# Six score banks in three chunks, a VectorE tile inside a unit, and new priorities in a hand-scheduled attention and feed-forward kernel

The kernel runs on one core of one Trainium2 chip. The metric is device time in microseconds; lower is better.

## The reference

A pre-norm transformer block without learned norm weights: 2048 tokens, width 640, 32 heads of 20, full attention, then a gated feed-forward of 1728. Cut to what matters:

```python
qkv = (layernorm(x) @ wqkv)            # [2048, 3*640]
scores = q @ k.T * 20 ** -0.5          # 32 heads, each 2048 x 2048
o = softmax(scores) @ v
h = x + o @ wo
g, u = layernorm(h) @ w_gate, layernorm(h) @ w_up
out = h + (gelu(g) * u) @ w_down
```

## The kernel before

The program is not written in issue order. It records operations with an estimated duration, a priority, reads, writes and PSUM banks; a list scheduler then fixes the order of each engine, and that static order is compiled. The queries come in seven chunks (512, 512, 256, 256, 256, 128, 128). A "tile" is one 128x512 fp32 score bank; there are 2048. Tiles are taken in "units":

```python
PAT = [((0, 1, 2), (3, 4))] * len(CHUNKS)      # units of three and of two banks, in turn
...
qk = op("pe", fns, 0.215, P_QK, mode="row", ..., acq=bks)          # scores of a unit
xd = dtile[u]
if xd:                                          # one more tile, for VectorE, in a background bank
    bd = Bank(*BG[slots[xd[0]][0]])
    qd = op("pe", [...], 0.08, P_QK + 0.5, mode="row", ..., acq=[bd], after=[qk])
...
exp_ops.append(op("act", I("activation", pt, PS[...], ACT.Exp, scale=SCALE), c_act(n), P_QK,
                  mode="exp", reads=[("S", u)], writes=pk, rel=bks[0:na], ...))
```

ScalarE takes one exp over a whole unit. About one tile in eight goes to VectorE instead, which evicts it from PSUM and forms its exp by a chain of seven cheap operations for each pair of tiles. Softmax needs no maximum pass, because a bound is folded into the QK.

The output projection, layer norm and feed-forward of a chunk are "background": they run on TensorE and VectorE between the QKs and PVs of later chunks, with the lowest priorities, and their gelus interrupt ScalarE once a chunk. What is left of them, and the last chunk's whole feed-forward, runs in a tail behind the last exp.

In the profiles, before / after the change: line 852 / 873 is QK, 1039 / 1061 gate and up, 1096 / 1118 down, 616 / 630 other projections, 812 / 830 VectorE's eviction of its score tile. Line 339 / 353 is the helper through which exps, PVs and most of VectorE are recorded. The tiles tell them apart: `pts` and `rege` hold the probabilities.

Of the kernel before, what the change touches and what calls it, by code (L numbers as in the profile page):

```python
# [17 lines left out]
WARM_WIN, WARM_MIN = 3.4, 0.5  # L18
PAD_WIN, PAD_MIN = 3.4, 0.42
PE_AGE = 1.5  # L20

MODE_SWITCH = {"pe": 0.105, "act": 1.28}

# [18 lines left out]
class Sched:  # L42
# [3 lines left out]
    def __init__(self, nc):  # L46
        self.nc = nc
        self.ops = []
        self.lw = {}
        self.rd = {}  # L50
        self.warm = None
        self.pad = None
        self.final = set()

    def op(self, eng, fns, dur, prio, reads=(), writes=(), acq=(), rel=(), after=(), sem=None, lat=None, mode=None, util=0.0):
        o = Op()
        o.i = len(self.ops)
# [28 lines left out]
    def schedule(self):  # L86
# [18 lines left out]
        t = 0.0  # L105
        recent = collections.deque()
        live = False
        total = len(ops)
        while done < total:
# [4 lines left out]
            for e in ENGINES:  # L114
# [8 lines left out]
                while ready[e]:  # L123
                    p, i = heapq.heappop(ready[e])
                    o = ops[i]
                    got = []
                    for bk in o.acq:
                        for b in bk.allowed:
                            if owner[b] is None and free_at[b] <= t + 1e-9 and b not in got and b not in kept:
                                got.append(b)  # L130
                                break
                        else:
                            got = None
                            break
# [50 lines left out]
                if e == "pe" and self.pad is not None and o.tag and o.tag[0] == "O":  # L185
                    while recent and recent[0][0] < t - PAD_WIN:
                        recent.popleft()
                    u = sum(x for _, x in recent) + o.util
                    while u < PAD_MIN * PAD_WIN and o.util < 1.1:
                        o.fns = o.fns + self.pad  # L190
                        o.dur += 0.215
                        o.util += 0.213
                        u += 0.213
                    live = o.i not in self.final
                o.start = t
                if o.util:
                    recent.append((t, o.util))
# [87 lines left out]
S = 2048  # L285
# [23 lines left out]
ND = 4  # L309
D_PER_SLOT = (8,) * len(SIZES)  # L310
D_SLOT0 = 2
D_FIRST, D_SPAN = 1, 16
RSQRT_MAGIC = float(0x5F3759DF)

P_QK, P_PV, P_PRO, P_EPI, P_LN, P_BG = 0, 1, 1.5, 2, 2.5, 3


def bass_sequential_preLN__mha_block__glu_gated_geglu__prompt_kernel(
# [12 lines left out]
    with ExitStack() as es:  # L331
# [10 lines left out]
        def c_mm(n, passes=1):  # L342
            return 0.001 + passes * n / 2400.0

# [420 lines left out]

        PAT = [((0, 1, 2), (3, 4))] * len(CHUNKS)
        units, ubank, dtile, ends = [], [], [], []
        i, in_slot = 0, {}
        while i < len(tiles):
# [5 lines left out]
            units.append(tiles[i:i + len(bs)])  # L775
            ubank.append(bs[0])
            i += len(units[-1])
            want = min(nd, (k[0] - D_FIRST) * nd // D_SPAN + 1) if k[0] >= D_FIRST else 0
            if k[1] < want and tiles[i][0] == s_:
                dtile.append(tiles[i])  # L780
# [50 lines left out]
        def unit(u):  # L831
# [10 lines left out]
            pt = pb[:, 512 * o:512 * (o + na)]  # L842
            bks = [Bank(s0 + i) for i in range(len(tl))]
            fns = []
            reads = []
            nkm = max(512 // CHUNKS[slots[x[0]][0]][1] for x in tl)

# [15 lines left out]
            for kk in range(nkm):  # L863
                for i, x in enumerate(tl):
                    if kk < 512 // CHUNKS[slots[x[0]][0]][1]:
                        fns.append(qk_mms(lambda i=i: PS[:, 512 * (s0 + i):512 * (s0 + i) + 512], x, kk))
                        reads += qk_reads(x)
            qk = op("pe", fns, 0.215, P_QK, mode="row", util=0.0533 * len(tl), reads=reads, writes=[("S", u), "qkseq"], acq=bks)
            for x in tl:
                last_qk[slots[x[0]][0]].append(qk)  # L870
            xd = dtile[u]
            if xd:
                bd = Bank(*BG[slots[xd[0]][0]])
# [73 lines left out]
        def epilogue(s_, bk):  # L947
# [13 lines left out]
            for tt in range(4):  # L961
                op("pe", lambda eng, tt=tt: eng.transpose(bank(b2)[:, tt * 128:(tt + 1) * 128],
                                                          osb[:, s, tt * 128:(tt + 1) * 128], identf[:]),
                   c_mm(128, 4), P_EPI, mode="full", reads=[("osb", s), "identf"], writes=[key], acq=[b2] if tt == 0 else [],
                   after=tuple(aft) if tt == 0 else ())
            bv = lambda: bank(b2).rearrange("p (t j e) -> p t j e", t=4, j=4)
            rcv = rc[:, s, :].rearrange("p (t j) -> p t j", t=4)
            op("dve", lambda eng: eng.reciprocal(rcv, bv()[:, :, :, DH]), 0.17, P_EPI, reads=[key], writes=[("rc", s)])
            for gi, g in enumerate(gs):
# [3 lines left out]
                    rcv[:, gi * nt:(gi + 1) * nt, :].unsqueeze(3).to_broadcast([128, nt, 4, DH]), ALU.mult),  # L973
                   c_dve(80 * nt), P_EPI, reads=[key, ("rc", s)], writes=[("on", g, tb + tt) for tt in range(nt)],
                   rel=[b2] if gi == len(gs) - 1 else [])
# [146 lines left out]
        for s_, (c, gs) in enumerate(slots):  # L1122
# [30 lines left out]
            if gs[-1] == NG - 1:  # L1153
                tail = c == len(CHUNKS) - 1
                post(c, ALLB if tail else BG[c + 1], tail)
                if not tail:
                    prefetch(c + 1)
# [30 lines left out]
```

## Time and profile before

| | us |
|---|---|
| median of the four runs of before (lowest) | 928.55 (927.12) |
| median without the slow run | 927.77 |
| span of the profiled run | 925.5 |

One of the four runs, 1389.24 us, was slow; the ratios leave it out. Five terms add up to the span, and they follow from the start times of ScalarE's records:

- the time until the first exp;
- the exps, each counted with its usual distance from start to start;
- the lateness: what exps start later than that behind another exp;
- the breaks, in which ScalarE loads tables and does the gelus of a chunk;
- the tail, behind the slot of the last exp.

### The profile page before, as it was taken

The numbers are of one execution on the slowest core, as the hardware profiler recorded it, in microseconds if no ns is written. First come the engines' busy times: TensorE is split into PE (matmuls) and PEld (weight loads), VectorE is DVE, ScalarE is ACT, GpSimd is POOL, SyncE is SP. The second block draws the span as 40 slices with busy tenths as digits, with TensorE's granted clock in tenths as the row PEclk, the third lists the DMA queues.
The fourth block names the chain that finished last, engine by engine and source line by source line (L and its number), as shares of the span: only waits on it lengthen the run. The fifth ranks groups of instructions, "written<-read, shape, count | busy, mean of one in ns | idle before, by whom it ended". The sixth has DMA issues, their size and how long they took to land.

```text
span 925.5 us, 23154 instructions
## 1 busy us (share of the span) xinstructions
PE 845.3 (91%) x10109; PEld 354.8 (38%) x10109; DVE 810.3 (88%) x1703; ACT 885.7 (96%) x801; POOL 35.1 (4%) x117
## 2 busy tenths in 40 slices
PE   3998999999998998999888999999989999999998
PEld 2432322222232222233233333344444445555667
DVE  8859999999898998888798997989998997998873
ACT  6899999999999999999999999999999999999962
POOL 5000000000001000000001000001000000000100
DMA  7301010322550000001021000010100000110000
GB/s 256 95 18 44 18 55 18 90 60 66 152 180 16 15 1 1 1 15 44 1 31 23 9 2 1 16 30 10 37 16 16 9 23 2 31 32 10 10 17 16
DMA packets 39517, 34.36 MB, mean 37 GB/s; under 512 B 19436, under 2 KB 36936, under 8 KB 39416
## 3 DMA queue, kind: packets, MB, share of 16 engines
q1 hardware_dynamic: 39416, 32.89, 12.7%
q8 instruction: 79, 1.29, 0.6%
q14 instruction: 22, 0.18, 0.1%
HBM read 20.12 MB, written 8.09 MB: 30 GB/s over the span
## 4 chain that ended last, share of the span: by engine, by line
ACT 72%; PE 14%; DVE 11%; issue 1%; POOL 0%; DMA 0%
ACT pts L339 46%; ACT rege L339 25%; PE ps L1039 4%; DVE qt_all L339 3%; PE ps L616 3%; PE ps L852 3%; PE ps L339 3%; DVE rege L339 2%; PE ps L1096 2%; DVE qt_all L812 1%; DVE rege L812 1%; DVE stats L339 1%; ACT L339 1%; DVE rege L1074 1%; PE ps L561 0%
## 5 line engine op out<-in xcount | busy, mean ns | idle before, releaser
L339 ACT ACTIVATE pts<-ps 128x1536 bf16<-128x1536 f32 x480 | 573.1, 1379 | 4.9 <-PE ps L852 3.7
L852 PE MATMUL ps<-qt_all,kt_all 32*128 32x256 bf16 (+2 forms) x3584 | 303.4, 289 | 43.2 <-ACT pts L339 27.5
L339 ACT ACTIVATE rege<-ps 128x1536 bf16<-128x1536 f32 x239 | 300.1, 1381 | 2.1 <-PE ps L339 1.5
L852 PEld LDWEIGHTS ps<-qt_all,kt_all 32*128 32x128 bf16 x3584 | 95.0, 92 | 276.8 <-ACT pts L339 160.8
L339 DVE TENSOR_TENSOR qt_all<-qt_all 128x1024 bf16<-128x1024 bf16 (+1 forms) x240 | 164.0, 683 | 3.4
L1039 PE MATMUL ps<-rege,regw 128*128 128x256 bf16 (+2 forms) x980 | 154.7, 290 | 9.9 <-ACT rege L339 4.2
L339 PE MATMUL ps<-pts,v_all 128*21 128x256 bf16 (+2 forms) x2098 | 138.8, 290 | 0.5 <-DVE rege L339 0.5
L812 DVE TENSOR_SCALAR rege<-ps 128x512 int16<-128x512 f32 x154 | 105.3, 685 | 27.6 <-PE ps L852 26.8
L339 DVE TENSOR_SCALAR qt_all<-qt_all 128x1024 bf16<-128x1024 int16 (+1 forms) x288 | 115.8, 417 | 2.5
L339 PE MATMUL ps<-rege,v_all 128*21 128x256 bf16 (+2 forms) x1294 | 113.3, 292 | 0.1
L1039 PEld LDWEIGHTS ps<-rege,regw 128*128 128x128 bf16 x980 | 72.5, 98 | 67.9 <-issue 28.5
L616 PE MATMUL ps<-regw 128*128 128x512 bf16 (+1 forms) x360 | 86.9, 351 | 1.9 <-DVE v_all L749 0.7
L1096 PE MATMUL ps<-regw,rege 128*128 128x320 bf16 x448 | 79.4, 301 | 1.1 <-DVE rege L1064 0.5
L812 DVE TENSOR_SCALAR qt_all<-ps 128x512 int16<-128x512 f32 x96 | 65.6, 684 | 3.7 <-PE ps L852 2.6
L339 DVE TENSOR_SCALAR rege<-rege 128x1024 int16<-128x1024 int16 (+2 forms) x166 | 67.1, 421 | 1.3
L339 DVE TENSOR_TENSOR rege<-rege 128x1024 bf16<-128x1024 bf16 (+3 forms) x103 | 65.5, 644 | 0.9
L339 PEld LDWEIGHTS ps<-pts,v_all 128*21 128x21 bf16 x2098 | 50.2, 91 | 37.2 <-issue 31.6
L339 PE MATMUL ps<-kt_all,zer 128*32 128x512 bf16 x676 | 56.6, 384 | 0.0
L1096 PEld LDWEIGHTS ps<-regw,rege 128*128 128x128 bf16 x448 | 36.7, 97 | 32.4 <-issue 15.8
L339 PEld LDWEIGHTS ps<-rege,v_all 128*21 128x21 bf16 x1294 | 41.0, 91 | 20.6 <-issue 14.3
L1085 DVE TENSOR_TENSOR rege<-rege,ps 128x512 bf16<-128x512 bf16 (+1 forms) x53 | 35.7, 676 | 12.1 <-PE ps L1039 11.8
L616 PEld LDWEIGHTS ps<-regw 128*128 128x128 bf16 x360 | 28.6, 98 | 45.2 <-issue 21.0
(95 smaller groups left out, 574.3 us busy)
## 6 DMA issues: line engine op xcount, KB each, us to landing
rege<-in_A_x_dram SPq DMA_DIRECT2D x6, 640.0 KB, 5.1
q_rows<-regw SPq DMA_DIRECT2D x20, 128.0 KB, 1.7
out_dram<-rege SPq DMA_DIRECT2D x16, 160.0 KB, 2.1
regw<-in_B_w_gate_dram SPq DMA_DIRECT2D x1, 2160.0 KB, 11.9
regw<-in_B_w_up_dram SPq DMA_DIRECT2D x1, 2160.0 KB, 16.9
regw<-in_B_w_down_dram SPq DMA_DIRECT2D x1, 2080.0 KB, 22.9
kt_all<-k_rows SPq DMA_DIRECT2D x12, 160.0 KB
qt_all<-q_rows SPq DMA_DIRECT2D x12, 160.0 KB
```

Of the source, the lines that this page charges most:

```text
L339: return lambda eng: getattr(eng, method)(*args, **kwargs)
L616: yield op("pe", lambda eng, l=l, r=r, k=k: eng.matmul(bank(bk, n), l, r, start=(k == 0), stop=(k == len(steps) - 1)), c_mm(n), prio, mode ...
L812: d_ops.append(op("dve", lambda eng: eng.tensor_scalar(v[:, 512 * h:512 * h + 512], bank(b), EXP_MUL, -32000.0, ALU.mult, ALU.max), c_dve( ...
L852: return lambda eng: eng.matmul(out()[:, kk * nq:(kk + 1) * nq], kt_all[32 * j:32 * j + 32, g, kt * 128:(kt + 1) * 128], qt_all[32 * j:32 ...
L1039: op("pe", lambda eng, a=a, f=f, fi=fi: eng.matmul(bank(bk)[:, fi * nq:(fi + 1) * nq], w[:, a, F0[f]:F0[f] + 128], hnT[:, a, 128 * tb:128 ...
L1074: cp.append(op("dve", lambda eng, bg=bg, fv=fv, w=w: eng.tensor_copy(fv, bank(bg, w)), c_dve(w), p, reads=[kg], writes=hkeys(k), rel=[bg], ...
L1085: hdone.append(op("dve", lambda eng, bu=bu, fv=fv, w=w: eng.tensor_tensor(fv, fv, bank(bu, w), ALU.mult), c_dve(w), p, reads=[ku] + hkeys( ...
L1096: op("pe", lambda eng, f=f, o=o, hf=hf, bk=bk: eng.matmul(bank(bk, 320), ha_f[:, o:o + 128], wd[:, f, hf * 320:(hf + 1) * 320], start=(f = ...
```

## The change

Its intent: larger units in chunks two to four (six score banks, the VectorE tile being the third bank of a unit, one bank left for background work); quicker return of background banks, by putting the VectorE operations that free a bank (and the reciprocal and normalisation that lead up to one) ahead of its exp chains; no other TensorE work in front of a QK that falls due ("clearance"); 12 instead of 16 VectorE tiles in the last chunk; and three new cost figures in the scheduler. The core of the diff, cuts marked:

```diff
+QK_LEAD = .65
-MODE_SWITCH = {"pe": 0.105, "act": 1.28}
+MODE_SWITCH = {"pe": .098, "act": 1.28}
...
+        if eng == "dve" and rel and prio > self.ev:      # P_EV = 1.8 once the first chunk is through
+            prio = self.ev
...
+                    if e == "pe" and due is not None and o.prio[0] > 0 and t < due < t + o.dur + (...):
+                        skipped.append((p, i))
+                        ...
+                        continue
...
+                if e == "act":
+                    due = t + o.dur + (0.905 if o.dur > 1.2 else 1.332) - QK_LEAD if o.mode == "exp" else None
...
-D_PER_SLOT = (8,) * len(SIZES)
+D_PER_SLOT = (8,8,8,8,8,8,6)
...
-            return 0.001 + passes * n / 2400.0
+            return 0.004 + passes * n / 2400.0
...
-        PAT = [((0, 1, 2), (3, 4))] * len(CHUNKS)
+        PAT = [((0, 1, 2), (3, 4, 5)) if c in (1,2,3) else ((0, 1, 2), (3, 4)) for c in range(len(CHUNKS))]
...
+            if six and k[1] < want and len(units[-1]) == 3 and units[-1][2][0] == s_:
+                dtile.append(units[-1].pop())
...
-                   c_mm(128, 4), P_EPI, mode="full", ...
+                   c_mm(128, 2.5), P_EPI, mode="full", ...
```

More of the change, by code (lines that the diff above doesn't have):

```diff
@@ L53, in __init__ @@
         self.final = set()
+        self.ev = 9
     def op(self, eng, fns, dur, prio, reads=(), writes=(), acq=(), rel=(), after=(), sem=None, lat=None, mode=None, util=0.0):
+        if eng == "dve" and rel and prio > self.ev:
+            prio = self.ev
         o = Op()
@@ L107, in schedule @@
         live = False
+        due = None
         total = len(ops)
@@ L126, in schedule @@
                     got = []
+                    if e == "pe" and due is not None and o.prio[0] > 0 and t < due < t + o.dur + (MODE_SWITCH[e] if mode[e] not in (None, o.mode) else 0):
+                        skipped.append((p, i))
+                        if len(skipped) >= 60:
+                            break
+                        continue
                     for bk in o.acq:
@@ L188, in schedule @@
                     u = sum(x for _, x in recent) + o.util
-                    while u < PAD_MIN * PAD_WIN and o.util < 1.1:
+                    room = due - t - MODE_SWITCH[e] if due is not None and due > t else 1e9
+                    while u < PAD_MIN * PAD_WIN and o.util < 1.1 and o.dur + 0.215 < room:
                         o.fns = o.fns + self.pad
@@ L313 @@
 RSQRT_MAGIC = float(0x5F3759DF)
+P_EV = 1.8
 P_QK, P_PV, P_PRO, P_EPI, P_LN, P_BG = 0, 1, 1.5, 2, 2.5, 3
@@ L776, in bass_sequential_preLN__mha_block__glu_gated_geglu__prompt_kernel @@
             ubank.append(bs[0])
+            six = len(PAT[c][1]) == 3
             i += len(units[-1])
             want = min(nd, (k[0] - D_FIRST) * nd // D_SPAN + 1) if k[0] >= D_FIRST else 0
-            if k[1] < want and tiles[i][0] == s_:
+            if six and k[1] < want and len(units[-1]) == 3 and units[-1][2][0] == s_:
+                dtile.append(units[-1].pop())
+                k[1] += 1
+            elif not six and k[1] < want and tiles[i][0] == s_:
                 dtile.append(tiles[i])
@@ L842, in unit @@
             pt = pb[:, 512 * o:512 * (o + na)]
-            bks = [Bank(s0 + i) for i in range(len(tl))]
+            xd = dtile[u]
+            six = xd and len(PAT[slots[tl[0][0]][0]][1]) == 3
+            al = tl + ([xd] if six else [])
+            bks = [Bank(s0 + i) for i in range(len(al))]
             fns = []
             reads = []
-            nkm = max(512 // CHUNKS[slots[x[0]][0]][1] for x in tl)
+            nkm = max(512 // CHUNKS[slots[x[0]][0]][1] for x in al)
             def qk_mms(out, x, kk):
@@ L863, in unit @@
             for kk in range(nkm):
-                for i, x in enumerate(tl):
+                for i, x in enumerate(al):
                     if kk < 512 // CHUNKS[slots[x[0]][0]][1]:
@@ L867, in unit @@
                         reads += qk_reads(x)
-            qk = op("pe", fns, 0.215, P_QK, mode="row", util=0.0533 * len(tl), reads=reads, writes=[("S", u), "qkseq"], acq=bks)
-            for x in tl:
+            qk = op("pe", fns, 0.215, P_QK, mode="row", util=0.0533 * len(al), reads=reads, writes=[("S", u), "qkseq"] + ([("SD", xd)] if six else []), acq=bks)
+            for x in al:
                 last_qk[slots[x[0]][0]].append(qk)
-            xd = dtile[u]
-            if xd:
+            if six:
+                bd = bks[2]
+            elif xd:
                 bd = Bank(*BG[slots[xd[0]][0]])
@@ L963, in epilogue @@
                                                           osb[:, s, tt * 128:(tt + 1) * 128], identf[:]),
-                   c_mm(128, 4), P_EPI, mode="full", reads=[("osb", s), "identf"], writes=[key], acq=[b2] if tt == 0 else [],
+                   c_mm(128, 2.5), P_EPI, mode="full", reads=[("osb", s), "identf"], writes=[key], acq=[b2] if tt == 0 else [],
                    after=tuple(aft) if tt == 0 else ())
@@ L967, in epilogue @@
             rcv = rc[:, s, :].rearrange("p (t j) -> p t j", t=4)
-            op("dve", lambda eng: eng.reciprocal(rcv, bv()[:, :, :, DH]), 0.17, P_EPI, reads=[key], writes=[("rc", s)])
+            op("dve", lambda eng: eng.reciprocal(rcv, bv()[:, :, :, DH]), 0.17, min(P_EPI, sc.ev), reads=[key], writes=[("rc", s)])
             for gi, g in enumerate(gs):
@@ L973, in epilogue @@
                     rcv[:, gi * nt:(gi + 1) * nt, :].unsqueeze(3).to_broadcast([128, nt, 4, DH]), ALU.mult),
-                   c_dve(80 * nt), P_EPI, reads=[key, ("rc", s)], writes=[("on", g, tb + tt) for tt in range(nt)],
+                   c_dve(80 * nt), min(P_EPI, sc.ev), reads=[key, ("rc", s)], writes=[("on", g, tb + tt) for tt in range(nt)],
                    rel=[b2] if gi == len(gs) - 1 else [])
@@ L1154, in bass_sequential_preLN__mha_block__glu_gated_geglu__prompt_kernel @@
                 tail = c == len(CHUNKS) - 1
+                sc.ev = P_EV
                 post(c, ALLB if tail else BG[c + 1], tail)
```

## The prediction

> **What bounds the kernel now.** I read the busy table, the chain of work that ended last, the ScalarE groups by form, the waits, and then the timeline behind the last exp.
>
> ```profile
> PE 845.3 (91%) x10109; PEld 354.8 (38%) x10109; DVE 810.3 (88%) x1703; ACT 885.7 (96%) x801; POOL 35.1 (4%) x117
> ACT 72%; PE 14%; DVE 11%; issue 1%; POOL 0%; DMA 0%
> ...
> L339 ACT ACTIVATE pts<-ps 128x1536 bf16<-128x1536 f32 x240 | 381.5, 1589 | 4.4 <-PE ps L852 3.7 <-PE ps L339 0.6
> L339 ACT ACTIVATE pts<-ps 128x1024 bf16<-128x1024 f32 x240 | 280.5, 1169 | 0.5 <-PE ps L339 0.4
> L339 ACT ACTIVATE rege<-ps 128x1536 bf16<-128x1536 f32 x120 | 190.9, 1591 | 2.1 <-PE ps L339 1.5 <-PE ps L852 0.7
> L339 ACT ACTIVATE rege<-ps 128x1024 bf16<-128x1024 f32 x119 | 139.2, 1170 | 0.0
> ```
>
> ScalarE is busy 96% and holds 72% of the chain; it runs 360 exps of three score banks and 359 of two. The durations overlap their neighbours, so the cost is the distance between starts: in the trace's single records a three-bank exp is most often followed after 1331 ns and a two-bank one after 904 ns. That makes 427 ns a bank and 50 ns for each instruction (904 - 2 x 427). From the starts the span of 925.5 us divides without remainder into five terms:
> - before the first exp: 35.7 us
> - exps at those distances: 360 x 1.331 + 359 x 0.904 = 803.7 us
> - lateness of exps behind exps, beyond those distances: 12.9 us. Of it 10.1 us is in 42 places of over 0.05 us, the rest is jitter of some 16 ns
> - five breaks in which ScalarE changes tables and does the gelus of a chunk: 9.2 + 9.2 + 6.1 + 6.0 + 6.3 = 36.8 us
> - from the end of the last exp's slot, at 889.1, to the end: 36.4 us
>
> So most of the kernel is a saturated ScalarE. What can move is the lateness (12.9) and the tail (36.4). The tail is not ScalarE's:
>
> ```profile
> 830.00:889.10 59.10, 55.70 (x1273) 35.80 (x1260) 51.85 (x109) 59.04 (x52) 3.36 (x14) 1.00 0.05 11
> 889.10:925.50 36.40, 31.04 (x431) 25.79 (x428) 14.63 (x35) 11.32 (x15) 0.00 (x0) 1.00 0.04 15
> ```
>
> The columns are us, then TensorE, its weight loads, VectorE, ScalarE and GpSimd busy, clock and DMA. Before 889.1 ScalarE is full; after it, TensorE is busy 31.0 of 36.4 us. The timeline shows with what:
>
> ```profile
> 887.57 3.43 PE L1096 MATMUL ps<-regw,rege 128*128 128x320 bf16 x24
> ...
> 891.16 0.45 PE L339 MATMUL ps<-pts,v_all 128*21 128x128 bf16 x17
> ...
> 894.02 1.29 PE L1039 MATMUL ps<-rege,regw 128*128 128x128 bf16 x20 [0.34 <-DVE rege L1074]
> ...
> 897.85 1.45 PE L1039 MATMUL ps<-rege,regw 128*128 128x128 bf16 x23
> ...
> 900.49 1.70 ACT L339 ACTIVATE rege<-rege 128x1792 bf16<-128x1792 bf16 x1 [2.86 <-DVE rege L1074]
> ...
> 902.25 2.96 PE L1039 MATMUL ps<-rege,regw 128*128 128x128 bf16 x50
> ...
> 911.02 7.20 PE L1039 MATMUL ps<-rege,regw 128*128 128x128 bf16 x126
> 918.74 3.98 PE L1096 MATMUL ps<-regw,rege 128*128 128x320 bf16 x28 [0.52 <-DVE rege L1064]
> ```
>
> L1096 is a down projection, L1039 gate or up. 24 down matmuls left over from the fifth chunk stand in front of the last PV; then comes the whole feed-forward of the sixth chunk (70 gate, 70 up, 28 down), because its gate was not done in time, and then that of the last chunk (140 and 28). The sixth chunk's gelu starts only at 900.5, so its up projection occupies TensorE from 902.25 on.
>
> **What the Trainium skill says.**
> - "ScalarE: Activation LUTs", "What ACT_TABLE_LOAD costs": 0.833 ns per element; 186 ns fixed, of which neighbours overlap by about 93 ns; some 2.66 us for a change of set. The slope agrees (427/512 = 0.834 ns). The fixed part measures 50 ns, not 93, and a change about 1.5 us: the first break, 9.21 us, less gelus of 7168 columns (7168 x 0.834 ns + 4 x 50 ns = 6.18 us), leaves 3.03 us for two. I use the trace.
> - "PSUM — Partial Sum Buffer", "The four PSUM rules": eight banks, a matmul's output at most one bank of 512 fp32 columns. The 1536-column exps agree: three banks. Now 5 banks hold scores, 1 PV sums, 2 background work; after the change, in three chunks, 6, 1 and 1.
> - "Perfetto Trace Analysis", "Matmuls": independent groups should rotate through banks so that evacuating one overlaps the next group. One background bank gives that up for those chunks. No run shows that price yet.
> - "TensorE: Matmul & The Clock Gate", "Wait — 56ns, not 53.3ns?": N/2.4 GHz plus about 2.5 ns. It agrees: 126 matmuls of 128 columns in 7.20 us, (7.20 - 0.22)/125 = 55.8 ns; 28 of 320 in 3.98 us, (3.98 - 0.30)/27 = 136 ns.
>
> **The change part by part.** I counted in the issue orders of both built programs.
>
> (a) Three and three banks in the second to fourth chunk. 719 exps become 704: 394 of three banks and 310 of two. The VectorE tile is now a unit's third bank, so such a unit still has a two-bank exp. The last chunk gives VectorE 12 tiles instead of 16, so ScalarE gets 1802 banks instead of 1798. Sum: 394 x 1.331 + 310 x 0.904 = 804.7 us, **+1.0 us**: 15 instructions saved are 0.75, four banks more cost 1.7. The regrouping by itself is worth nothing that can be seen.
>
> (b) VectorE loses four evictions and two chains of seven steps, one for each pair of tiles; by the groups (685 ns an eviction, three steps at 0.68 and four at 0.42 a pair) some 9 us less of busy time, all in the last chunk. VectorE is not the bound; it only clears the last PV's inputs earlier.
>
> (c) Operations that free a bank now precede the exp polynomials on VectorE, from the first chunk's end on. With a queue 88% busy, that shortens the return of background banks. The orders show the sum of (a) to (c) on the background work: the fifth chunk's gelu now comes with 39 exps still to go instead of 27, and behind the last QK only about two matmuls of the sixth chunk's gate remain, and none of the fifth chunk's down. **Tail:** 24 x 0.136 + 70 x 0.056 = 3.3 + 3.9 = 7.2 us of TensorE work leave it. Are they on its path? Stepwise from the end E of the last exp: last PV 0.3 to 1.5, copy to 2.3, transposes and normalisation to 4.0, second transposes and their ScalarE eviction to 5.4, output projection to 7.0. Gelu needs one load and 1.7 us and is done by about 3 to 4, so the up projection (50 x 0.056 = 2.8) runs at 7 to 10 beside the layer norm; 28 down, 5 transposes and waits bring TensorE to about 14.2; then 140 x 0.056 = 7.9, a 0.5 us product, 28 x 0.136 = 3.8, and 2.8 us from the last matmul to the end as before: 29.2, say **29.5 us** against 36.4. One table load fewer (15 for 16) is in that. The gain is **-6.9 us**.
>
> (d) TensorE may not begin other work that would overrun a due QK. It aims at lateness such as the 0.37 us at 534.9, where 25 PV matmuls ran ahead of a QK. Against it, TensorE has more to do before E: work other than QK between QKs rises from 404 to 416 us by the counts (7.2 from the tail, some 4 us of fillers), and gaps between QKs holding over 0.75 us of work go from 155 to 189. I take 11 us for 12.9, **-1.9 us**.
>
> (e) Head and five breaks: the same instructions, so 35.7 and 36.8.
>
> Sum: 35.7 + 804.7 + 11 + 36.8 + 29.5 = 917.7 us of span. The profiled run before took 927.45 for a span of 925.5, 1.95 more, which gives 919.6; I say **919.5 us**, 1.1% below 929.32.
>
> **The rivals.**
> - *The single bank becomes the wait.* Matmuls into bank 7, eviction and return run in series, TensorE stands in order behind them, QKs come late. For it: the chunk-three gelu moves from 13 to 39 exps into the fifth chunk, so background work does lag there; and waits on evictions exist already (below). Against: the order places QKs between, and the work fits. At 0.1 us in a quarter of the 341 exps of those chunks it costs 8 us: 927.
>
> ```profile
> PEld ps L616 <- DVE rege L812: 5.7, 16, 0.7
> PEld ps L1039 <- DVE qt_all L812: 5.0, 13, 0.7
> DVE rege L812 <- PE ps L852: 26.8, 35, 3.5
> ```
>
> - *VectorE's third bank holds up the next QK.* The bank is free only after VectorE's eviction (0.685 us, behind an operation of up to 0.7), where before it was ScalarE's own. For: 128 units are of this kind. Against: the two-bank exp beside it lasts 0.9 and the next one 1.33, so there is slack of about one exp. If it failed, 128 x 0.05 us = 6 us: 925.
> - *The clearance rule works fully.* The 42 large places vanish and only 3 us of jitter stay: 911 to 912.
> - *The tail is bound by its chain, not by TensorE.* Then only half of the 7 us returns: 923.
>
> **Range and chances.** Tail 28 to 33 and lateness 4 to 16 give 911 to 928 at the extremes together; eight in ten is **913 to 926**. Faster by over 2% means under 910.7, which needs nearly all lateness gone besides the whole tail gain: 0.06. Slower by over 2% needs 948, some 28 us of new waits: 0.03. Within 2%: 0.91.
>
> **What would show it.** In the changed profile: 704 exps with starts 1331 and 904 ns apart; first exp at 35 to 36; last exp's end at 887 to 890, hardly moved; no 24 down matmuls ahead of the last PV, gelu of the sixth chunk within 5 us of the last exp, and a tail of 28 to 31 us; lateness 9 to 13 us. Wrong if lateness in chunks two to four grows beyond its present 5 us or so (single bank or VectorE bank), if the tail stays above 33, or if the last exp ends before 884, which would mean the clearance rule is worth more than I gave it.

## More of the kernel before

An exp writes probability tiles into a ring of buffers, which the PV matmuls read later:

```python
PR, PR2 = 12, 6                                 # probability buffers: 12 in pts, 6 in rege
...
if p0 < PR < p0 + na: p0 = PR                   # a unit does not straddle the two parts
if p0 + na > PR + PR2: p0 = 0
...
pv = op("pe", fns, 0.218 * len(quads), P_PV, mode="col", ..., reads=reads, writes=[("O", s_), "pvseq"])
```

## The result

The changed kernel took 923.94 us (median of 4 runs, 923.76 to 924.54) against 928.55 us. The ratio is 0.9957, with a 95% interval of 0.9937 to 0.9976: the same within 2%, but a clear gain of some 0.4%. Ratios here are the mean time of one kernel's fast runs over the mean of the other's fast runs of the same rounds, so they are not quite the ratios of the medians. The time lies in the predicted range; the gain is less than half of the 1.1% forecast. That 1.1% was taken from 929.32 us, the median of the three runs then known, of which one was the slow one; in spans of profiled runs, which leave this aside, 7.8 us were forecast and 3.7 came.

| us | before | after | difference | predicted difference |
|---|---|---|---|---|
| until the first exp | 35.7 | 36.3 | +0.6 | 0 |
| exps | 803.7 | 804.7 | +1.0 | +1.0 |
| lateness | 12.9 | 13.8 | +0.9 | -1.9 |
| breaks | 36.8 | 37.3 | +0.4 | 0 |
| tail | 36.4 | 29.8 | -6.6 | -6.9 |
| span | 925.5 | 921.8 | -3.7 | -7.8 |

From the page of the changed kernel, the busy table and the engines of the chain that ended last:

```profile
PE 821.2 (89%) x10080; PEld 351.1 (38%) x10141; DVE 805.5 (87%) x1685; ACT 885.8 (96%) x785; POOL 35.7 (4%) x117
...
ACT 70%; PE 16%; DVE 12%; issue 1%; DMA 1%; POOL 0%
```

ScalarE is as busy as it was (885.8 us against 885.7). Its groups by form, after (count, busy us, mean ns, idle before and who ended it):

```profile
L353 ACT ACTIVATE pts<-ps 128x1536 bf16<-128x1536 f32 x263 | 403.8, 1585 | 5.8 <-PE ps L873 4.5 <-PE ps L353 0.9
L353 ACT ACTIVATE pts<-ps 128x1024 bf16<-128x1024 f32 x211 | 243.0, 1152 | 0.2
```

With the other 131 and 99 these are the 394 and 310 exps that were counted. The tail changed as planned. The two windows, up to the last exp and from it to the end (columns as in the prediction):

```profile
832.60:892.00 59.40, 55.70 (x1255) 37.82 (x1257) 45.65 (x93) 58.33 (x51) 2.57 (x14) 1.00 0.05 14
892.00:921.80 29.80, 24.29 (x344) 20.20 (x345) 11.18 (x28) 9.96 (x14) 0.00 (x0) 1.00 0.04 13
```

TensorE has 24.3 us of work behind the last exp where it had 31.0. The timeline of the tail, after:

```profile
892.35 0.62 PE L353 MATMUL ps<-pts,v_all 128*21 128x128 bf16 x32 [1.42 <-ACT pts L353]
...
893.61 1.70 ACT L353 ACTIVATE rege<-rege 128x1792 bf16<-128x1792 bf16 x1
...
898.95 2.99 PE L1061 MATMUL ps<-rege,regw 128*128 128x128 bf16 x50
...
906.55 7.98 PE L1061 MATMUL ps<-rege,regw 128*128 128x128 bf16 x140
...
915.05 3.98 PE L1118 MATMUL ps<-regw,rege 128*128 128x320 bf16 x28 [0.52 <-DVE rege L1086]
```

The last PV starts 0.33 us after the last exp's slot, where 24 down matmuls had stood in front of it; the sixth chunk's gelu starts at 893.6, 1.6 us after it (11.4 us before: 900.5 less 889.1); no gate of the sixth chunk is left.

The lateness has to be looked at one exp at a time. For each exp at least 0.05 us late I matched the operations it waits for with their records: its own QK, and the PVs that last read the buffers that it overwrites. The later of them is what held it. Before, 39 late exps waited for their QK (6.9 us) and 4 for a PV (3.3 us); after, 47 for their QK (8.6 us) and 5 for a PV (3.7 us); what is left, 2.8 and 1.5 us, is in smaller pieces. The longest before was a wait for a PV, too, and stood in the timeline that was read for the prediction:

```profile
144.17 1.45 ACT L339 ACTIVATE rege<-ps 128x1536 bf16<-128x1536 f32 x1 [1.46 <-PE ps L339]
```

The longest after:

```profile
834.69 0.40 PE L873 MATMUL ps<-qt_all,kt_all 32*128 32x128 bf16 x12
...
835.70 0.39 PE L353 MATMUL ps<-rege,v_all 128*21 128x128 bf16 x8
836.03 0.40 PE L873 MATMUL ps<-qt_all,kt_all 32*128 32x128 bf16 x8
836.13 2.37 ACT L353 ACTIVATE pts<-ps 128x1536 bf16<-128x1536 f32 x2 [0.94 <-PE ps L353]
```

The scores were there at about 835.1, but the exp starts at 836.13, behind the PV that ends at 836.09. The releaser, line 353, is a PV and not a QK. By chunk the lateness, in us, is 5.0, 2.4, 2.3, 1.1, 1.2, 0.6, 0.3 before and 3.8, 2.9, 1.5, 0.9, 1.0, 1.8, 1.9 after. In chunks two to four, where the pattern changed, it fell a little in sum (though not in chunk two). It grew by 2.9 us in the last two chunks, where the work that left the tail now lies; 2.1 us of this are two exps, at 810.06 and 836.13, that wait for a slot's last PV of 48 matmuls.

### The profile page after: what moved, and what is told of

Its sections match the earlier page's. It is cut to its first block, busy times and chain, and to the rows that moved or that the text cites. A ratio compares the mean times of both kernels' runs of the same rounds, so it can differ in the third digit from the quotient of the medians.

```text
span 921.8 us, 23227 instructions
## 1 busy us (share of the span) xinstructions
PE 821.2 (89%) x10080; PEld 351.1 (38%) x10141; DVE 805.5 (87%) x1685; ACT 885.8 (96%) x785; POOL 35.7 (4%) x117
## 3 DMA queue, kind: packets, MB, share of 16 engines
q1 hardware_dynamic: 39416, 32.89, 12.9%
## 4 chain that ended last, share of the span: by engine, by line
ACT 70%; PE 16%; DVE 12%; issue 1%; DMA 1%; POOL 0%
ACT pts L353 44%; ACT rege L353 24%; PE ps L873 4%; DVE qt_all L353 4%; PE ps L353 3%; PE ps L630 3%; PE ps L1061 3%; PE ps L1118 2%; DVE rege L353 2%; ACT L353 1%; DVE rege L830 1%; DVE rege L1096 1%; DVE qt_all L830 1%; DVE stats L353 1%; PE ps L575 0%
## 5 line engine op out<-in xcount | busy, mean ns | idle before, releaser
L353 ACT ACTIVATE pts<-ps 128x1536 bf16<-128x1536 f32 (+1 forms) x474 | 574.7, 1392 | 6.0 <-PE ps L873 4.5
L873 PE MATMUL ps<-qt_all,kt_all 32*128 32x256 bf16 (+2 forms) x3584 | 287.7, 289 | 55.7 <-ACT pts L353 32.0
L353 ACT ACTIVATE rege<-ps 128x1536 bf16<-128x1536 f32 (+1 forms) x230 | 293.9, 1398 | 2.0 <-PE ps L353 1.2
L873 PEld LDWEIGHTS ps<-qt_all,kt_all 32*128 32x128 bf16 x3584 | 90.4, 92 | 276.9 <-ACT pts L353 163.6
L353 DVE TENSOR_TENSOR qt_all<-qt_all 128x1024 bf16<-128x1024 bf16 (+1 forms) x235 | 161.2, 686 | 4.1
L1061 PE MATMUL ps<-rege,regw 128*128 128x256 bf16 (+2 forms) x952 | 151.2, 287 | 14.8 <-ACT rege L353 4.7
L353 PE MATMUL ps<-pts,v_all 128*21 128x256 bf16 (+2 forms) x2122 | 136.1, 290 | 2.3 <-ACT pts L353 1.4
L353 PE MATMUL ps<-rege,v_all 128*21 128x256 bf16 (+2 forms) x1278 | 108.0, 292 | 0.0
L630 PE MATMUL ps<-regw 128*128 128x512 bf16 (+1 forms) x341 | 81.6, 351 | 3.0 <-DVE rege L830 1.2
L1118 PEld LDWEIGHTS ps<-regw,rege 128*128 128x128 bf16 x448 | 36.5, 98 | 32.4 <-issue 14.1
L353 PEld LDWEIGHTS ps<-rege,v_all 128*21 128x21 bf16 x1278 | 39.2, 91 | 19.4 <-issue 13.8
```

The source lines that it names most:

```text
L353: return lambda eng: getattr(eng, method)(*args, **kwargs)
L630: yield op("pe", lambda eng, l=l, r=r, k=k: eng.matmul(bank(bk, n), l, r, start=(k == 0), stop=(k == len(steps) - 1)), c_mm(n), prio, mode ...
L873: return lambda eng: eng.matmul(out()[:, kk * nq:(kk + 1) * nq], kt_all[32 * j:32 * j + 32, g, kt * 128:(kt + 1) * 128], qt_all[32 * j:32 ...
L1061: op("pe", lambda eng, a=a, f=f, fi=fi: eng.matmul(bank(bk)[:, fi * nq:(fi + 1) * nq], w[:, a, F0[f]:F0[f] + 128], hnT[:, a, 128 * tb:128 ...
L1118: op("pe", lambda eng, f=f, o=o, hf=hf, bk=bk: eng.matmul(bank(bk, 320), ha_f[:, o:o + 128], wd[:, f, hf * 320:(hf + 1) * 320], start=(f = ...
```

## The experiments

All gave correct outputs. In each table "behind PV" is the part of the lateness, in places of 0.05 us or more, in which a PV came last. For orientation: before is 925.5 in span with 12.9 of lateness, 3.3 behind PV, last exp's end 889.1, tail 36.4; the change is 921.8, 13.8, 3.7, 892.0, 29.8. The spans come from one profiled run each; the part before the first exp varied from 35.0 to 36.5 over all profiles, so a span's difference below 1.5 us says little.

### First round: one part out, or one part alone

**The changed kernel without the clearance rule.**

```diff
-                    due = t + o.dur + (0.905 if o.dur > 1.2 else 1.332) - QK_LEAD if o.mode == "exp" else None
+                    due = None
```

> The changed kernel with the clearance rule for due QKs taken out, all else kept. Theory A (the gain is the tail's alone; lateness is decided by how much other TensorE work is packed between the QKs, and the rule only moves it about): lateness of exps 12 to 16 us beside 13.8 with the rule, tail 29 to 31, span 921 to 925. Theory B (the rule pays as I predicted, and the single background bank eats its gain): lateness 16 us or more, span above 925.

**The changed kernel without the priority.**

```diff
-                sc.ev = P_EV
```

> The changed kernel without the priority for VectorE operations that free a bank. Theory A (this priority is what brings the background work forward, and so the tail): tail back to 33 to 38 us, span 926 to 933. Theory B (the tail gain comes from the twelve instead of sixteen VectorE tiles in the last chunk): tail stays at 29 to 31, span 920 to 924.

**The kernel before with the regrouping alone**: the change with the clearance, the priority, the twelve tiles and the cost figures undone.

```diff
+        PAT = [((0, 1, 2), (3, 4, 5)) if c in (1,2,3) else ((0, 1, 2), (3, 4)) for c in range(len(CHUNKS))]
+            if six and k[1] < want and ...: dtile.append(units[-1].pop())      # and its QK, as in the change
```

> The kernel before with three and three score banks in chunks two to four and nothing else of the change. Theory A (regrouping gives nothing by itself and the single background bank makes background work fall behind): last exp ends some us earlier because work is pushed out, tail above 42 us, span 930 to 942. Theory B (the regrouping is a gain by itself: fewer, larger exps): tail at most 37, lateness 10 to 12, span 918 to 924.

**The kernel before with the clearance rule alone**: the lines with `due` and `room` of the diff, and nothing else.

```diff
+                    if e == "pe" and due is not None and o.prio[0] > 0 and t < due < t + o.dur + (...):
+                        skipped.append((p, i)); ...; continue
```

> The kernel before with the clearance rule and nothing else. Theory A (in the three and two pattern the rule holds TensorE back where it has no slack to give): lateness 15 to 22 us, against 12.9, and span 928 to 938. Theory B (my prediction's step d): lateness at most 11, span at most 924.

| run | median us | ratio (95%) | span | lateness | behind PV | last exp's end | tail |
|---|---|---|---|---|---|---|---|
| after_no_clearance | 924.00 | 0.9962 (0.9947 to 0.9977) | 921.7 | 14.0 | 4.9 | 891.6 | 30.1 |
| after_no_priority | 932.66 | 1.0054 (1.0039 to 1.0069) | 930.2 | 15.2 | 4.0 | 894.4 | 35.8 |
| before_33_only | 942.15 | 1.0165 (1.0133 to 1.0197) | 941.4 | 16.5 | 5.1 | 886.3 | 55.1 |
| before_clearance_only | 938.63 | 1.0124 (1.0106 to 1.0142) | 934.5 | 26.8 | 17.1 | 902.3 | 32.2 |

Theory A held on tails; its lateness for the rule alone was well short. Inside the change the clearance rule is worth nothing: without it the waits for QKs are 7.3 us (8.6 with it) and those behind PVs 4.9 (3.7). The priority carries the tail: without it the tail is 35.8 us, though the last chunk still has twelve VectorE tiles. Regrouping alone is the slowest kernel of the round: with one background bank and no priority the background work falls so far behind that only four of the five gelu breaks fit before the last exp, and the tail becomes 55.1 us. These two conditions are not enough for that, however: after_no_priority has both, and a tail of 35.8. What the twelve tiles, the rule and the cost figures, or merely another order, do to prevent it is not divided. The window behind the last exp of before_33_only:

```profile
886.30:941.40 55.10, 51.03 (x605) 42.40 (x602) 25.26 (x53) 14.47 (x17) 1.97 (x11) 1.00 0.07 22
```

The clearance rule alone was the surprise: lateness doubles, and nearly all of the excess is behind PVs. ScalarE's waits in that run (us in total, times, longest):

```profile
ACT pts L353 <- PE ps L353: 8.9, 8, 1.8
...
ACT pts L353 <- PE ps L873: 4.5, 3, 3.7
ACT rege L353 <- PE ps L353: 4.2, 3, 1.8
```

The QK line includes 3.7 us before the very first exp; the two PV lines add up to 13.1 us where they were 1.5 and 0.9 before. One of them in the timeline:

```profile
513.39 0.39 PE L873 MATMUL ps<-qt_all,kt_all 32*128 32x256 bf16 x6
...
513.71 0.39 PE L1061 MATMUL ps<-rege,regw 128*128 128x512 bf16 x1
514.04 0.65 PE L873 MATMUL ps<-qt_all,kt_all 32*128 32x256 bf16 x6
514.62 0.62 PE L353 MATMUL ps<-pts,v_all 128*21 128x256 bf16 x16
...
515.28 0.39 PE L353 MATMUL ps<-rege,v_all 128*21 128x256 bf16 x4
...
515.71 1.45 ACT L353 ACTIVATE pts<-ps 128x1536 bf16<-128x1536 f32 x1 [1.80 <-PE ps L353]
```

TensorE issues the exp's own QK, a gate matmul and the next QKs first; the exp's own QK is through 1.9 us before the exp starts, but the PV that must empty its buffers (24 matmuls) comes after them all. A PV has a priority number above 0, so the rule holds it back like any background work. Late PVs have been added, and late QKs have not gone: the waits for QKs are 7.4 us here and 6.9 before.

### Second round: which parts need each other

**Three and two banks again, without the clearance rule, the rest of the change kept.**

```diff
-        PAT = [((0, 1, 2), (3, 4, 5)) if c in (1,2,3) else ((0, 1, 2), (3, 4)) for c in range(len(CHUNKS))]
+        PAT = [((0, 1, 2), (3, 4))] * len(CHUNKS)
-                    due = t + o.dur + ... if o.mode == "exp" else None
+                    due = None
```

(With the clearance rule this kernel cannot be built: the scheduler stops because nothing wakes TensorE when the due time is reached, and no other event happens to.)

> The changed kernel with three and two score banks in all chunks again and without the clearance rule (which made no difference inside the change); the priority, the lighter last chunk and the new cost figures stay. Theory A2 (regrouping pays only together with the priority, because larger units leave TensorE longer stretches for the background work): span 928 to 938, with a tail as short as 28 to 31 us but a last exp ending at 897 or later. Theory B2 (regrouping costs by its single background bank, and the priority alone would do better): span 916 to 921, lateness at most 13 us.

**The kernel before with the priority alone.**

```diff
+        if eng == "dve" and rel and prio > self.ev:
+            prio = self.ev
+                sc.ev = P_EV
```

> The kernel before with the priority for bank-freeing VectorE operations and nothing else. Theory A2 (needs the regrouping): tail 30 to 33 us, but the last exp ends at 896 or later, since the work it pulls ahead of the last exp has no room there; span 926 to 933. Theory B2 (the priority is the whole gain): tail 30 to 33, last exp at 889 to 892, span 919 to 924.

**The kernel before with regrouping and priority**: the two edits together.

> The kernel before with regrouping and priority together, nothing else. Theory A2: these two are the core; tail 35 to 40 us against 55 with regrouping alone, last exp at 891 to 896, span 926 to 933; what still lacks against the change is the last chunk's lighter VectorE load and the cost figures. Theory B2: still as slow as regrouping alone, 938 or more.

**The changed kernel with 16 VectorE tiles in the last chunk.**

```diff
-D_PER_SLOT = (8,8,8,8,8,8,6)
+D_PER_SLOT = (8,8,8,8,8,8,8)
```

> The changed kernel with 16 instead of 12 VectorE tiles in the last chunk. ScalarE has four banks less to do (1.7 us); VectorE some 9 us more in the last 50 us. If VectorE's chains bound the start of the tail, tail 32 to 36 us and span 923 to 927; if not, tail 29 to 31 and span 919 to 921.

| run | median us | ratio (95%) | span | lateness | behind PV | last exp's end | tail |
|---|---|---|---|---|---|---|---|
| after_32_no_clearance | 938.93 | 1.0124 (1.0109 to 1.0139) | 935.9 | 25.8 | 15.8 | 908.9 | 27.0 |
| before_priority_only | 930.99 | 1.0048 (1.0031 to 1.0064) | 928.9 | 21.0 | 11.8 | 898.1 | 30.8 |
| before_33_priority | 933.19 | 1.0065 (1.0046 to 1.0085) | 929.6 | 17.4 | 7.7 | 892.7 | 36.9 |
| after_16_tiles_last | 925.03 | 0.9975 (0.9960 to 0.9990) | 923.5 | 14.4 | 4.6 | 891.1 | 32.4 |

The priority alone does what it is meant to do, a tail of 30.8 us, and loses more than that by late exps, again behind PVs. The lighter last chunk shortens the tail by 2.6 us and costs 1.8 us of ScalarE. The tail of 27.0 us in after_32_no_clearance is short because the sixth chunk's gelu came before the last exp there, in a sixth break of 4.6 us. With three and three banks the PV waits shrink. My explanation then (larger units leave TensorE longer stretches) fitted the numbers, but there is a simpler one in the buffer ring. Units of three and two fill 3+2+3+2 = 10 of the twelve buffers and 3+2 = 5 of the six, so three of eighteen stay empty; six units of three would fill all eighteen. In the change it is not quite that, since a unit with a VectorE tile has an exp of two banks: counted from the code, 3.0 buffers stay empty in each round of the ring before, and 1.6 to 1.9 in chunks two to four after.

### Third round: the probability buffers

Two more buffers fit into SBUF. Twenty, as 13 and 7, are filled exactly by eight units of three and two (3+2+3+2+3 and 2+3+2). The edit of the first three runs is the same, on top of before, of the clearance rule alone and of the priority alone:

```diff
-PR, PR2 = 12, 6
+PR, PR2 = 13, 7
```

> The kernel before with twenty instead of eighteen probability buffers (13 and 7 for 12 and 6), nothing else. Units of three and two leave three of the eighteen unused (3,2,3,2 in twelve, 3,2 in six: six units in flight); twenty are filled by eight units. Theory R (in the three and two pattern exps wait for PVs to have read the buffers that they write; that is the hidden limit on all that the change does): the 3.3 us of such waits vanish, background work may be done earlier beside it, span 918 to 922, as much as the whole change gained. Rival Q (PV waits are incidental, TensorE is simply full): span within 2 us of 925.5.

> The kernel before with the clearance rule and twenty probability buffers. With eighteen the rule alone had 26.8 us of lateness, 17.1 of it behind PVs. Theory R: lateness 10 to 16 us, with under 5 behind PVs, span 922 to 928. Rival Q (the rule wastes TensorE time whatever the buffers): lateness 22 us or more, span above 930.

> The kernel before with the priority and twenty probability buffers, still three and two. With eighteen the priority alone had 21.0 us of lateness, 11.8 behind PVs. Theory R (regrouping helps the priority because six units of three fill the buffers; more buffers do the same): lateness 11 to 15, span 920 to 924. Theory A2 as first put (larger units leave TensorE longer stretches): lateness stays at 18 or more, span above 926.

**A candidate**: the change without its clearance rule, with twenty buffers and a slot's last PV cut up.

```diff
-                fns, reads = [], ["vones", "zer"] + k_keys[0][0]
-                for have in quads:
+                for q0_ in range(0, len(quads), 2):
+                    fns, reads = [], ["vones", "zer"] + k_keys[0][0]
+                    for have in quads[q0_:q0_ + 2]:
...
+                    pv = op("pe", fns, ...)        # one operation for each piece
```

> A candidate for better than both: the changed kernel without the clearance rule, with twenty probability buffers, and with the last PV of a slot cut into operations of at most two quads, so that a QK can go between. Theory R: lateness 9 to 11 us against 14.0, waits behind PVs under 1.5 us, tail 30 to 31, span 914 to 918. Rival Q: lateness 13 or more, span 920 to 923.

| run | median us | ratio (95%) | span | lateness | behind PV | last exp's end | tail |
|---|---|---|---|---|---|---|---|
| before_ring20 | 922.96 | 0.9948 (0.9929 to 0.9966) | 921.0 | 11.2 | 0 | 888.4 | 32.7 |
| before_clearance_ring20 | 931.78 | 1.0035 (1.0012 to 1.0059) | 931.2 | 18.8 | 0.4 | 895.8 | 35.5 |
| before_priority_ring20 | 924.17 | 0.9960 (0.9945 to 0.9975) | 921.8 | 13.7 | 3.0 | 889.5 | 32.4 |
| split_ring20_33 | 919.53 | 0.9919 (0.9898 to 0.9940) | 917.5 | 9.7 | 0 | 887.7 | 29.8 |

Two more buffers in the kernel before, one line, give as much as the whole change. Of the 4.5 us of span only 1.7 are lateness: the waits behind PVs went (-3.3), those for QKs grew from 6.9 to 8.8. (The longest place of before, 1.57 us at 144.2, is still there, at 141.9 and as long, but behind its QK.) The tail, in another order, gave 3.7, and the head took 0.8. Its waits of exps, from ScalarE's waits:

```profile
ACT pts L339 <- PE ps L852: 4.9, 2, 3.7
...
ACT rege L339 <- PE ps L852: 0.3, 1, 0.3
```

No exp waits for a PV any more. The priority's lateness falls from 21.0 to 13.7 with the buffers, without any regrouping, which the theory of longer stretches does not explain. The clearance rule's PV waits go from 17.1 to 0.4 us, but both theories missed its total: QK waits rise to 16.7, from 8.8 without the rule. Of these 2.4 us, two exps at 306.4 and 309.8, fall where the granted clock was halved (304.3 to 311.2; this profile has three such falls between its first exp and its end, that of before_ring20 none); another, 1.2 us at 302.8, came just before. The windows there:

```profile
302.00:306.00 4.00, 2.76 (x23) 0.74 (x24) 3.88 (x9) 2.37 (x2) 0.00 (x0) 0.79 0.21 41
306.00:310.00 4.00, 4.00 (x18) 0.74 (x17) 3.32 (x7) 2.66 (x3) 0.00 (x0) 0.50 0.00 0
```

The rest stands: even with buffers enough the rule made the kernel before slower (931.78 against 922.96), with more waits for QKs and not fewer. That the time in which TensorE is held back is the reason is argued, not isolated.

The candidate is the fastest kernel so far, but three things differ from the change at once. What the cut PV gives was not run alone.

### Fourth round: the cause in the changed kernel itself, and the rest

**The changed kernel with twenty buffers**: the same one-line edit.

> The changed kernel with twenty probability buffers and nothing else. Theory R (PV waits are what kept its lateness from falling to the predicted 11): waits behind PVs under 1 us against 3.7, lateness 10 to 12, the last exp's end at 888 to 890. The order moves with it, so the tail may grow to 33; span 920 to 923. Rival Q: lateness stays at 13 to 15.

**Three and two banks with everything that helps**: the split and the twenty buffers on the change, with 16 VectorE tiles throughout, and the rule at a lead of 0.40 with the missing wake-up.

```diff
+        PAT = [((0, 1, 2), (3, 4))] * len(CHUNKS)
+PR, PR2 = 13, 7
+QK_LEAD = .4
+MODE_SWITCH = {"pe": .095, "act": 1.28}
+                if wk and chosen is None:           # wk: work was skipped for a due QK
+                    heapq.heappush(events, due)
```

> Three and two score banks everywhere, twenty probability buffers, PV in pieces of at most two quads, the priority, a clearance lead of 0.40 us with a wake-up of TensorE when the QK is due, 16 VectorE tiles in every slot. Theory R (regrouping only made up for buffers that three and two fills badly): span 913 to 918, as good as the three and three version with twenty buffers (917.5) or better, lateness 8 to 11. Rival (larger units are worth something of their own): span 921 or more.

**The changed kernel with the old cost figures** (0.105, 0.001 and four passes).

```diff
-MODE_SWITCH = {"pe": .098, "act": 1.28}
+MODE_SWITCH = {"pe": 0.105, "act": 1.28}
...
-            return 0.004 + passes * n / 2400.0
+            return 0.001 + passes * n / 2400.0
...
-                   c_mm(128, 2.5), P_EPI, mode="full"
+                   c_mm(128, 4), P_EPI, mode="full"
```

> The changed kernel with the scheduler's three cost figures as before. If they matter only through the order they happen to give, lateness and tail both move by a few us: lateness 16 to 22, tail 30 to 33, span 928 to 934. If they are a detail: span within 2 us of 921.8.

**The changed kernel with a lead of 0.60 instead of 0.65 us.**

```diff
-QK_LEAD = .65
+QK_LEAD = .60
```

> The changed kernel with a lead of 0.60 instead of 0.65 us. If the result is a property of the rule, span within 2 us of 921.8. If it is a property of the one order that 0.65 gives, several us away: last exp at 902 to 906 with a tail of 28 to 29, span 929 to 934.

| run | median us | ratio (95%) | span | lateness | behind PV | last exp's end | tail |
|---|---|---|---|---|---|---|---|
| after_ring20 | 922.68 | 0.9945 (0.9930 to 0.9960) | 920.4 | 10.8 | 0.4 | 888.8 | 31.6 |
| split_ring20_32 | 920.01 | 0.9921 (0.9902 to 0.9940) | 918.0 | 11.6 | 0 | 888.1 | 29.9 |
| after_old_costs | 931.37 | 1.0035 (1.0018 to 1.0052) | 929.8 | 20.9 | 10.8 | 898.0 | 31.8 |
| after_lead60 | 936.12 | 1.0091 (1.0075 to 1.0106) | 933.8 | 23.6 | 14.0 | 905.3 | 28.5 |

With two more buffers the changed kernel has 10.8 us of lateness, 0.4 of it behind PVs. ScalarE's waits for PVs in the changed kernel,

```profile
ACT rege L353 <- PE ps L353: 1.2, 2, 0.7
...
ACT pts L353 <- PE ps L353: 0.9, 1, 0.9
```

have no counterpart among those of after_ring20; there only the QK lines are left:

```profile
ACT pts L353 <- PE ps L873: 4.5, 3, 3.7
...
ACT rege L353 <- PE ps L873: 0.6, 2, 0.4
```

The tail gives back 1.8 us, because the order moves, so that the span gains no more than 1.4 us. With enough buffers three and two banks everywhere do as well as three and three (918.0 and 917.5), though with a lateness of 11.6 us, above the 8 to 11 expected. The two kernels differ in the rule, its wake-up, the last chunk's tiles and a cost figure as well, so this compares two tuned kernels and not one edit. A gain of larger units as such is not seen; that the regrouping only made up for badly filled buffers fits, and is not isolated. The last two runs are a warning: 0.05 us in the rule's lead, or the old cost figures (7 and 3 ns for a change of mode and a matmul, and the estimate of one transpose), cost 7 to 12 us, and in both the added lateness is behind PVs. (after_lead60 has a sixth break of 4.6 us besides, and a tail that is shorter for it.) Whether this sensitivity goes with twenty buffers was not run.

## Why the prediction was wrong

**Right.** The ledger itself, and step (a): the exps grew by 1.0 us, as worked out. Step (c) was right in mechanism and nearly in size: the tail is 29.8 us for 29.5 predicted, and its stations are those listed (last PV from 0.33 to 1.4 us after the last exp, output projection done at 7.1, background down done at 14.7). One part taken out at a time, the tail loses 6.0 us of this with the priority (35.8 without it) and 2.6 with the lighter last chunk, which step (b) had named but not priced; together that is more than the whole, so the two are no shares. The sum in (b) is slightly off: four evictions and two chains at its own figures are 10.2 us, not some 9, which changes nothing else.

**Wrong: step (d), "I take 11 us for 12.9, -1.9 us".** It measured 13.8, +0.9. This is 2.8 of the 4.1 us missed in the span. The head (+0.6) and the breaks (+0.4), taken as fixed in step (e), and 0.3 in the tail are the rest; the head's 0.6 is within its variation. Two things failed in (d).

- *The rule does not shorten the waits that it aims at.* I counted it as a gain for late QKs. These waits rose from 6.9 to 8.6 us, and without the rule the changed kernel has 7.3 and the same lateness (14.0). In all three pairs of kernels that differ in the rule alone they are longer with it (without and with it 6.9 and 7.4, 8.8 and 16.7, 7.3 and 8.6; of the 16.7, 2.4 lie where the clock was halved). More than that, in all twelve kernels with eighteen buffers, with the rule or without, they lie between 6.7 and 9.9 us. Why the rule fails to shorten them is open; step (d) had named the greater load of TensorE as a counterweight, but not tested it.
- *Lateness is not lateness of QKs alone.* I took it to be that from the one example at 534.9 (0.37 us is ScalarE's idle time there, 0.63 us the lateness from start to start, and 24 PV matmuls, not 25, run ahead). At 144.2, the longest of all (1.57 us), ScalarE had already been waiting for a PV, and the timeline named it. The rule holds back PVs as well: alone it raised the waits behind them from 3.3 to 17.1 us. Over the twelve kernels it is this part that varies, from 3.3 to 17.1 us.

What keeps the waits behind PVs up is the ring of eighteen probability buffers: with twenty, and nothing else changed, they fell in all four kernels (3.3 to 0, 17.1 to 0.4, 11.8 to 3.0, 3.7 to 0.4). This brought the changed kernel to 10.8 us of lateness. That it is the size which I had predicted is luck: the waits for QKs, which step (d) meant to shorten, are still 8.3 us there. The ring explains the level of the lateness and not its rise by 0.9, which comes mostly from QKs (+1.7).

**The rivals.** The single background bank did not hold up exps: lateness in chunks two to four fell from 5.9 to 5.2 us, and with the regrouping alone it is 6.7. In that kernel it went with background work pushed far back (tail 55.1), but after_no_priority, with one background bank and no priority either, has 35.8. VectorE's third bank did not hold them up either, by the same 5.2 us. The full success of the clearance rule did not come. The chain did not bind the tail beyond what was counted. The waits behind PVs, 3.3 us before and 3.7 after, stood on no list of mine.

**What stays open.** How much of each part's effect belongs to the part, and how much to the one order in which the scheduler happened to put some 3500 TensorE operations, cannot be told below some 10 us from single variants: after_lead60 and after_old_costs keep every part and are 12 and 8 us slower in span. That buffers are a limit does not hang on one order: with twenty, the lateness fell in all four kernels in which only they were changed. But these runs add two buffers and fill the three that stood empty at once, and do not tell the two apart.

The best version measured is split_ring20_33, at 919.53 us, 0.8% below before and 0.5% below the change (917.5 against 921.8 in span); split_ring20_32, 920.01 us, is level with it.

## What to carry to other kernels

Split the lateness of a saturated engine by what ended each wait before changing priorities: here two kinds, late inputs and buffers not yet emptied, looked alike in the busy table, and in the kernel before a rule against the first fed the second and left the first as it was. Check how a ring of buffers is filled by the sizes that really come, since a pattern can leave a sixth of it empty; here twenty buffers, all filled, were worth as much as the whole scheduling change. Where a scheduler makes the order, test a result against small neutral changes of its parameters before crediting a part of the change with it.

## What the Trainium skill lacked or had wrong

- "ScalarE: Activation LUTs", "What ACT_TABLE_LOAD costs": it gives some 2.66 us for each change of table set. Here a change costs about 1.5 us (a break of 9.21 us with 6.18 us of gelus and two changes).
- "Perfetto Trace Analysis", "Optimization Strategy": it says that consistent bubbles on the engine that should be saturated can mean too few buffers. Here the missing buffers showed as 4 to 14 single waits of up to 4.8 us among some 700 exps in the twelve kernels with eighteen buffers, not as a repeating gap; two more buffers removed 3.3 us of them in the kernel before.
- "Perfetto Trace Analysis", "Matmuls": it advises independent matmul groups to rotate through banks. The loss of rotation for background work did not show as waits of the bound engine in the changed kernel (5.2 us of lateness in those chunks against 5.9). With the regrouping alone it went with work pushed behind the last exp, 55.1 us of tail against 36.4, and with bank-freeing VectorE work put first the tail was 36.9; each is one order of one scheduler.
- "TensorE: Matmul & The Clock Gate", "What's actually happening": it speaks of a return to half clock after an idle window of about 3.4 us. In before_clearance_ring20 the granted clock was 0.50 from 304.3 to 311.2, though in the 3.4 us before that TensorE's records were busy 1.91 us with no gap over 1.25; in after_old_costs, at 459.4, they were busy 2.18 us with no gap over 0.63. In these places partly busy stretches were enough; the page gives no share of busy time at which the clock falls.
